# Attention on one core: the preparing transposes of keys and queries, and the products with the values, dealt anew over the nine loops of a head pair

## The chip, the cores and the metric

One Trainium2 chip, one core of it. The metric is device microseconds (us) of one execution of the whole program, lower is better. The kernel before took 1369.54 us, the median of three runs (1367.63 to 1370.73).

## The reference

The program computes three stages, one after the other: attention with pooled queries, a dense two-layer network with an ELU between the layers, and a routed network of eight experts. The change touches the attention alone:

```python
B, H, S, D = q.shape                                   # 4, 8, 1152, 64
q_pool = q.reshape(B, H, S // 2, 2, D).mean(axis=3)    # 576 queries per head
scores = 1/np.sqrt(D) * np.matmul(q_pool, k.transpose(0, 1, 3, 2))
scores = scores - np.max(scores, axis=-1, keepdims=True)
attn = np.exp(scores)
attn = attn / (np.sum(attn, axis=-1, keepdims=True) + 1e-09)
return np.matmul(attn, v).astype(np.float32)           # 1152 keys, 64 columns
```

## The kernel before, in words

**Pairs and tiles.** Two heads make a pair; there are 16 pairs (0 to 15). A pair has 2 x 576 queries, which are nine tiles of 128. Tiles 0 to 3 belong to the first head, tiles 5 to 8 to the second, and tile 4 is the middle tile, half of either. Every float32 factor is split into a high and a low part, so that products of float32 accuracy come out of several passes.

**One loop per tile.** The loop of lines 251 to 287 runs over all 144 tiles, nine loops to a pair; I write loop t for t = 0 to 8 within a pair. SEQ (line 17) is the order in which one loop emits its work, and since each engine takes its own instructions in that order, it also is each engine's order. One loop works at three depths:

- scores of the tile two ahead (`qk`, line 144; `q1` writes the last third of the keys to `Sb`, `q0` the first two thirds to `Sa`), their maxima on VectorE (`smax`, line 147, `nm<-Sb`, `nm<-Sa`; `bias`, line 150) and the exponentials on ScalarE (`exp`, line 154, `P<-Sa` and `P<-Sb`). A target tile 4 needs both heads' keys and so twelve products where the others need six; it is emitted in loop 2. `Sa` has one buffer in PSUM (CFG S2=1): the next `Sa` waits until the exponential has read the last one.
- the tile itself: its probabilities P are transposed in three groups of three (`tp`, line 187) into PSUM tiles `T`, and each group is taken out as a high part by ScalarE (`evH`, line 198, `PH<-T`) and a low part by VectorE (`evL`, line 200, `PL<-T,PH`). In loop 4, the middle tile, each takes two instructions for a group instead of one.
- products with the values of query chunks that are complete (`av`, line 210, `O<-PH,vs` and `O<-PL,vs`). A chunk has 18 of them, four chunks make 72 to a pair. AVN (line 18) says how many each loop emits. Loops 0 to 4 work on chunks of 256 columns, loops 5 to 8 on chunks of 320.

**What is prepared for the next pair.** The scores need transposed keys and queries. `kop` (lines 92 to 99) transposes a third of one head's keys: three transposes into a `T`, and one copy by ScalarE into `kst` (line 98). k00, k01, k02 are the thirds of the first head, k10, k11, k12 those of the second. `qop` (lines 101 to 118) does the same for thirds of the queries (line 105, copies in line 106), and after q2 two DMAs on SyncE's queue fill the second layout (lines 116, 117). PREP (line 19) says which of these each loop emits, late in its order (`prep`), behind the products with the values. The pair number there is relative: (0, ...) is this pair, (1, ...) the next. In loops 3 and 7 one more transpose follows, that of the inverse sums (`invT`, line 165, `T<-ident,rc`).

**The T buffers.** All of these, three P groups a loop, preparing thirds and `invT`, take their PSUM tile `T` from one pool of three buffers (CFG T=3) in turn. The fourth taken in a loop needs the first one's readers done, and so on.

**When the thirds are needed.** Loop 7 emits the first scores of the next pair (all k0 thirds and all q thirds), `Sb` first. Loop 2 emits the middle tile's scores, which need the k1 thirds: `Sb` with k12 first, then `Sa` with k10 and k11. Before, k12 is transposed at the end of loop 1 of its own pair.

**Extra work.** From the 71st loop on the loops also carry weight decoding for the next stage (lines 309 to 323, mostly VectorE), in pairs 8 to 12, and later splitting of its inputs.

Of the kernel before, what the change touches and what calls it, by code (L numbers as in the profile page):

```python
# [14 lines left out]


SEQ='q1 q0 m1 sum dec t0 c0 m0 pool scl t1 c1 bias l0 t2 av c2 l1 e0 e1 l2 aw prep inv st'.split()
AVN=(8,10,4,9,5,8,10,10,8)
PREP={0:((0,'k11'),(1,'q0')),1:((0,'k12'),),3:((1,'q1'),),4:((1,'q2'),(1,'k00'),(1,'k01')),5:((1,'k02'),),8:((1,'k10'),)}
POOL={0:((0,'vH1'),(0,'vL1')),1:((1,'kH0'),),2:((1,'kL0'),),4:((1,'kH1'),),5:((1,'kL1'),),6:((2,'qadd'),),7:((2,'qH'),(2,'qL')),8:((1,'vH0'),(1,'vL0'))}  # L20
SCALE=(7,8,11,12)
CFG=dict(S2=1,S1=2,T=3,O=1)
def attention(tc, q, k, v, xS, rS, ident, pairs=None, extra=(), start=lambda: None):
    nc=tc.nc
    B,H,S,D=q.shape
# [3 lines left out]
    with ctx:  # L29
# [4 lines left out]
        kv=ctx.enter_context(tc.tile_pool(name="a_kv",bufs=1))  # L34
# [53 lines left out]
        def prep_ops(i):  # L88

            d=D_[i]  # L90
            ops=[]
            def kop(h,g):
                def f():
                    if g==0: d['kst'][h]=kv.tile([128,S],F32R,name="kst",tag="kst",bufs=2)
                    T=psT.tile([128,384],F32,name="T",tag="T")
                    for j in range(3):
                        nc.tensor.transpose(T[:,j*128:(j+1)*128],d['ks'][h][:,3*g+j].rearrange("p a d -> p (a d)").bitcast(F32),ident)
                    nc.scalar.copy(out=d['kst'][h][:,g*384:(g+1)*384],in_=T)
                return f
            A=QA[i%2]; Bq=QB[i%2]  # L100
            def qop(g):
                def f():
                    T=psT.tile([128,384],F32,name="T",tag="T")
                    for j in range(3):
                        nc.tensor.transpose(T[:,j*128:(j+1)*128],d['qsp'][:,3*g+j].rearrange("p a d -> p (a d)").bitcast(F32),ident)
                    cp=lambda o,i: nc.scalar.activation(out=o,in_=i,func=AF.Copy,scale=SC)
                    if g==0: cp(A[:,0:384],T)
                    elif g==2: cp(A[:,896:1280],T)
                    else:
                        w=T.rearrange("p (c x) -> p c x",c=3)  # L110
                        cp(A[:,384:1152].rearrange("p (c x) -> p c x",c=2)[:,:,0:128],w[:,0::2])
                        cp(A[:,512:768].rearrange("p (y x) -> p y x",x=64)[:,0::3],w[:,1].rearrange("p (a x) -> p a x",a=2))

                    sl=(slice(0,384),slice(384,896),slice(896,1280))[g] if i==0 else slice(0,1280)
                    if g==2 or i==0:
                        nc.sync.dma_start(out=Bq[0:64,sl].bitcast(F32),in_=A[64:128,sl].bitcast(F32))
                        nc.sync.dma_start(out=Bq[64:128,sl].bitcast(F32),in_=A[0:64,sl].bitcast(F32))
                return f
            return {f'q{g}':qop(g) for g in range(3)}|{f'k{h}{g}':kop(h,g) for h in range(2) for g in range(3)}
# [77 lines left out]
        def evH(g,j):  # L197
            for H,L,src in parts(g,j): nc.scalar.copy(out=H,in_=src)  # L198
        def evL(g,j):
            for H,L,src in reversed(list(parts(g,j))): nc.vector.tensor_tensor(out=L,in0=src,in1=H.bitcast(F32),op=ALU.subtract)  # L200
# [28 lines left out]
        def do(i,*names):  # L229

            if i>=N: return
            if i not in ops: ops[i]=pool_ops(i,i==0)|prep_ops(i)
            for n in names:
                o=ops[i].pop(n,None)
                if o: o()
# [10 lines left out]
        def takeav(n):  # L246
            if avq:
                take(avq[0],n)
                if not avq[0]: avq.pop(0)
        stores=[]; sums={}  # L250
        for g in range(NG+4):
# [8 lines left out]
            for op in SEQ:  # L260
# [15 lines left out]
                elif a=='c': evH(g,int(n))  # L276
                elif op in ('av','aw'): takeav((AVN[t]+(op=='av'))//2)
                elif a=='l': evL(g,int(n))
                elif op=='sum':
                    if t in (3,7): ssum(i,t//4)  # L280
                elif op in ('pool','prep'):
                    for di,n in (POOL if op=='pool' else PREP).get(t,()): do(i+di,n)
                elif op=='dec':
# [706 lines left out]
```

## Time and profile before

| what | value |
|---|---|
| median of three runs | 1369.54 us |
| the profiled execution's own time | 1370.3 us |
| its span in the trace | 1368.5 us |
| PE (TensorE) busy, share of the span | 1242.2 us, 91% |
| PEld (weight loads, overlap PE) | 1098.8 us, 80% |
| DVE (VectorE) busy | 1099.7 us, 80% |
| ACT (ScalarE) busy | 907.4 us, 66% |
| POOL (GpSimd) busy | 625.6 us, 46% |

The attention's score products begin 12 us into the span and its last score maximum lies at about 584 us. Times of the trace are counted from the start of the span. A row of the timeline has its start, its length, the engine, the line of the kernel, the operation, the names that it writes and reads, and the number of like instructions that were merged; in brackets how long the engine was idle before it and who ended that. Matmuls are pipelined: their lengths overlap, and the distance from one start to the next is what each costs. In the text T(t) is the start of the nine transposes of loop t.

### The profile page before, as it was taken

How to read it: one execution, taken by the hardware profiler on the slowest of the kernel's cores; microseconds unless marked ns; L12 is line 12 of the kernel's file. 1: busy time of each engine (PE TensorE's matmuls, PEld its weight loads, DVE VectorE, ACT ScalarE, POOL GpSimd, SP SyncE). 2: the span in 40 equal slices, each digit the busy share in tenths (PEclk: the TensorE clock that was granted, in tenths of full speed). 3: DMA queues.
4: the chain of work that ended last, by engine and by line, in shares of the span. 5: the costliest groups of instructions: out<-in, count | busy, mean ns of one | idle time of the engine just before them, and what ended most of it. 6: DMA issues, size and time to landing. Idle time of an engine off the chain costs nothing. (4 is left out here: it accounts for less than half of the span.)

```text
span 1368.5 us, 22229 instructions
## 1 busy us (share of the span) xinstructions
PE 1242.2 (91%) x7476; PEld 1098.8 (80%) x7476; DVE 1099.7 (80%) x1970; ACT 907.4 (66%) x2104; POOL 625.6 (46%) x537
## 2 busy tenths in 40 slices
PE   5999999999999899977777999899989999999997
PEld 4988898888888888875565988797979887788885
DVE  5778887778888887879999497939395889998993
ACT  6888888887888788844444645454555666666772
POOL 4444444444444355336666543434342344545662
PEclk9999999999999999999999999999999999999998
DMA  5334333334443254233432311110100314348810
GB/s 157 98 106 107 106 107 106 103 100 114 113 113 105 83 142 113 62 118 94 127 99 73 110 32 35 32 34 22 33 24 17 154 50 159 100 161 326 298 35 21
DMA packets 78342, 136.62 MB, mean 100 GB/s; under 512 B 9255, under 2 KB 52663, under 8 KB 73872
## 3 DMA queue, kind: packets, MB, share of 16 engines
q1 hardware_dynamic: 73952, 123.22, 30.1%
q0 software_dynamic: 3696, 11.34, 2.4%
q8 instruction: 61, 1.00, 0.3%
q10 hardware_dynamic: 576, 0.59, 0.1%
q14 instruction: 57, 0.47, 0.1%
HBM read 155.48 MB, written 20.28 MB: 128 GB/s over the span
## 5 line engine op out<-in xcount | busy, mean ns | idle before, releaser
L399 PE MATMUL h<-xH,W 128*128 128x384 f32 (+1 forms) x896 | 229.2, 327 | 55.0 <-ACT yt L408 39.5
L198 ACT CAST PH<-T 128x384 fp32r<-128x384 f32 (+1 forms) x480 | 182.6, 460 | 94.5 <-PE T L187 92.5
L399 PEld LDWEIGHTS h<-xH,W 128*128 128x128 f32 x896 | 161.9, 195 | 77.0 <-ACT yt L408 50.2
L200 DVE TENSOR_TENSOR PL<-T,PH 128x384 fp32r<-128x384 f32 (+1 forms) x480 | 216.0, 509 | 1.3 <-ACT PH L198 1.3
L422 POOL TENSOR_TENSOR gL<-et,gH 128x384 fp32r<-128x384 f32 (+1 forms) x112 | 119.4, 1066 | 199.5 <-ACT gH L421 174.1
L787 DVE TENSOR_TENSOR W<-sg,W 128x2048 fp32r<-128x2048 f32 (+1 forms) x84 | 190.4, 2299 | 17.7 <-ACT W L786 9.8
L404 ACT ACTIVATE em<-h 128x384 f32<-128x384 f32 (+1 forms) x112 | 49.9, 445 | 224.9 <-DVE et L413 155.7
L210 PE MATMUL O<-PH,vs 128*128 128x256 f32 (+1 forms) x576 | 167.2, 313 | 0.6 <-ACT xo L213 0.6
L187 PE MATMUL T<-ident,P 128*128 128x128 f32 x1296 | 165.3, 273 | 0.0
L147 DVE TENSOR_REDUCE nm<-Sa 128x1 f32<-128x768 f32 x144 | 137.3, 954 | 29.7 <-PE Sa L144 18.6
L210 PE MATMUL O<-PL,vs 128*128 128x256 f32 (+1 forms) x576 | 157.6, 297 | 0.0
L187 PEld LDWEIGHTS T<-ident,P 128*128 128x128 f32 x1296 | 150.6, 141 | 5.1
L399 PE MATMUL h<-xL,W 128*128 128x384 f32 (+1 forms) x448 | 143.6, 321 | 0.0
L147 DVE TENSOR_REDUCE nm<-Sb 128x1 f32<-128x384 f32 x144 | 80.2, 557 | 72.8 <-PE Sb L144 72.2
L154 ACT ACTIVATE P<-Sa,bs 128x768 f32<-128x768 f32 x144 | 133.7, 929 | 7.0 <-DVE bs L150 6.6
L413 DVE SCALAR_TENSOR_TENSOR et<-em,et 128x384 f32<-128x384 f32 (+1 forms) x112 | 69.5, 621 | 83.9 <-ACT em L410 82.3
L144 PE MATMUL Sa<-kst,qa 128*128 128x384 f32 x320 | 111.1, 347 | 18.9 <-ACT P L154 18.8
L786 ACT CAST W<-sg 128x2048 fp32r<-128x2048 f32 (+1 forms) x63 | 114.3, 1836 | 12.7 <-DMA sg<-moe_w 12.7
L215 POOL TENSOR_TENSOR xo<-xo,rB 128x256 f32<-128x256 f32 (+1 forms) x64 | 52.2, 819 | 152.3 <-ACT xo L213 82.1
L430 PE MATMUL y<-W,gH 128*128 128x512 f32 x288 | 114.8, 398 | 0.0
L431 PE MATMUL y<-W,gH 128*128 128x512 f32 x288 | 113.2, 393 | 0.0
L210 PEld LDWEIGHTS O<-PH,vs 128*128 128x128 f32 x576 | 108.7, 189 | 1.1 <-ACT xo L213 0.8
(295 smaller groups left out, 3058.4 us busy)
## 6 DMA issues: line engine op xcount, KB each, us to landing
sg<-moe_w SPq DMA_DIRECT2D x80, 1024.0 KB
qb<-qa SPq DMA_DIRECT2D x30, 320.0 KB
qn<-q SPq DMA_DIRECT2D x16, 576.0 KB
kn<-k SPq DMA_DIRECT2D x16, 576.0 KB
rB<-rS SPq DMA_DIRECT2D x32, 288.0 KB
vn<-v SPq DMA_DIRECT2D x15, 576.0 KB
dx<-moe_w_in SPq DMA_DIRECT2D x16, 512.0 KB
dx<-moe_w_out SPq DMA_DIRECT2D x16, 512.0 KB
```

The lines of the kernel that those rows point to most:

```text
L147: nc.vector.tensor_reduce(out=s['nm'][:,n:n+1],in_=s['S'][n],axis=AX.XY if n==0 else AX.X,op=ALU.max,negate=True)
L154: nc.scalar.activation(out=o,in_=s['S'][n],func=AF.Exp,bias=s['bs'],scale=1.0,accum_out=s['su'][:,n:n+1])
L187: nc.tensor.transpose(T[:,n*128:(n+1)*128],P[:,kt*128:(kt+1)*128],ident)
L198: for H,L,src in parts(g,j): nc.scalar.copy(out=H,in_=src)
L200: for H,L,src in reversed(list(parts(g,j))): nc.vector.tensor_tensor(out=L,in0=src,in1=H.bitcast(F32),op=ALU.subtract)
L210: nc.tensor.matmul(O[0][:,:n],vs[:,kt].rearrange("p a d -> p (a d)"),R[:,kt,:n],start=first,stop=last)
L399: nc.tensor.matmul(h[:,:N],a,b[:,k,:N],start=(n==0),stop=(n==11)); n+=1
L422: nc.gpsimd.tensor_tensor(out=gL[:,:N],in0=t_,in1=gH[:,:N].bitcast(F32),op=ALU.subtract)
L430: nc.tensor.matmul(y,gH[:,sl],wH,start=(f==0),stop=False)
L431: nc.tensor.matmul(y,gH[:,sl],wL,start=False,stop=False)
L786: else: nc.scalar.copy(out=H[:,q],in_=s[:,q])
L787: (nc.gpsimd if (w,j,h) in self.pool_L else nc.vector).tensor_tensor(out=L[:,q],in0=s[:,q],in1=H[:,q].bitcast(F32),op=ALU.subtract)
```

## The change

PREP and AVN get other entries, and `kop` makes its `kst` tile at the first third that is emitted, whichever that is, since a pair's thirds no longer come in the order of their number.

```diff
-AVN=(8,10,4,9,5,8,10,10,8)
-PREP={0:((0,'k11'),(1,'q0')),1:((0,'k12'),),3:((1,'q1'),),4:((1,'q2'),(1,'k00'),(1,'k01')),5:((1,'k02'),),8:((1,'k10'),)}
+AVN=(7,11,0,5,13,8,10,9,9)
+PREP={0:((0,'k11'),(1,'q0')),1:((1,'q1'),),2:((1,'q2'),),3:((1,'k02'),(1,'k00')),5:((1,'k01'),),7:((1,'k12'),),8:((1,'k10'),)}
...
-                    if g==0: d['kst'][h]=kv.tile([128,S],F32R,name="kst",tag="kst",bufs=2)
+                    if h not in d['kst']: d['kst'][h]=kv.tile([128,S],F32R,name="kst",tag="kst",bufs=2)
```

By loops:

| loop | prepared before | prepared after | products with values before | after |
|---|---|---|---|---|
| 0 | k11, q0 | k11, q0 | 8 | 7 |
| 1 | k12 | q1 | 10 | 11 |
| 2 | none | q2 | 4 | 0 |
| 3 | q1 | k02, k00 | 9 | 5 |
| 4 | q2, k00, k01 | none | 5 | 13 |
| 5 | k02 | k01 | 8 | 8 |
| 6 | none | none | 10 | 10 |
| 7 | none | k12 | 10 | 9 |
| 8 | k10 | k10 | 8 | 9 |

## Rows read from the trace of the kernel before

**Rows 1.** Stretches: length, busy PE PEld DVE ACT POOL, granted clock, DMA share, GB/s

```profile
128.00:304.70 176.70, 166.50 (x1212) 156.35 (x1209) 140.95 (x305) 146.37 (x411) 74.91 (x77) 1.00 0.38 103
...
304.70:489.32 184.62, 169.22 (x1211) 156.43 (x1210) 155.00 (x326) 149.76 (x415) 81.62 (x78) 1.00 0.40 110
```

**Rows 2.** Waits from 15 to 584 us: total, times, longest

```profile
POOL qsp L65 <- PE T L105: 82.9, 11, 12.6
...
PE Sb L144 <- ACT kst L98: 14.2, 15, 1.0
...
PE T L105 <- DVE PL L200: 6.0, 17, 0.7
```

**Rows 3.** TensorE's timeline, pair 7, loops 1 to 3

```profile
273.16 1.14 PE L187 MATMUL T<-ident,P 128*128 128x128 f32 x9
...
275.80 0.33 PE L144 MATMUL Sb<-kst,qb 128*128 128x384 f32 x1
277.08 0.44 PE L144 MATMUL Sb<-kst,qa 128*128 128x384 f32 x1 [0.95 <-ACT kst L98]
...
278.92 1.15 PE L187 MATMUL T<-ident,P 128*128 128x128 f32 x9
...
281.64 0.44 PE L144 MATMUL Sa<-kst,qa 128*128 128x384 f32 x1 [0.76 <-ACT P L154]
...
282.44 1.14 PE L187 MATMUL T<-ident,P 128*128 128x128 f32 x9
283.34 0.36 PE L210 MATMUL O<-PH,vs 128*128 128x256 f32 x1
...
284.37 0.28 PE L210 MATMUL O<-PH,vs 128*128 128x256 f32 x1
284.49 0.49 PE L105 MATMUL T<-ident,qsp 128*128 128x128 f32 x3
...
284.84 0.42 PE L144 MATMUL Sb<-kst,qa 128*128 128x384 f32 x1
```

**Rows 4.** TensorE's timeline, pair 7, loops 4 and 5

```profile
285.98 1.14 PE L187 MATMUL T<-ident,P 128*128 128x128 f32 x9
...
288.02 0.52 PE L105 MATMUL T<-ident,qsp 128*128 128x128 f32 x3 [0.32 <-DVE PL L200]
288.55 1.05 PE L97 MATMUL T<-ident,ks 128*128 128x128 f32 x6
...
290.48 1.14 PE L187 MATMUL T<-ident,P 128*128 128x128 f32 x9
```

**Rows 5.** TensorE's timeline, pair 0, scores of the middle tile

```profile
28.30 0.34 PE L144 MATMUL Sb<-kst,qb 128*128 128x384 f32 x1
28.48 0.34 PE L144 MATMUL Sb<-kst,qa 128*128 128x384 f32 x1
```

**Rows 6.** ScalarE's timeline, pair 7, loops 2 and 4

```profile
279.45 1.25 ACT L198 CAST PH<-T 128x384 fp32r<-128x384 f32 x3 [2.42 <-PE T L187]
...
281.36 0.22 ACT L154 ACTIVATION_READ_ACCUMULATOR P<-Sa,bs 128x1 f32 x1
...
288.57 0.25 ACT L154 ACTIVATION_READ_ACCUMULATOR P<-Sa,bs 128x1 f32 x1
```

**Rows 7.** VectorE's timeline, pair 7, loops 3 and 4

```profile
281.58 0.55 DVE L147 TENSOR_REDUCE nm<-Sb 128x1 f32<-128x384 f32 x1
...
282.64 0.96 DVE L147 TENSOR_REDUCE nm<-Sa 128x1 f32<-128x768 f32 x1
...
283.71 1.48 DVE L200 TENSOR_TENSOR PL<-T,PH 128x384 fp32r<-128x384 f32 x3
...
287.25 1.68 DVE L200 TENSOR_TENSOR PL<-T,PH 128x192 fp32r<-128x192 f32 x6
```

**Rows 8.** Stretches again: loop 4 of pair 7, and an early stretch of pair 0

```profile
285.90:289.40 3.50, 3.16 (x26) 2.54 (x24) 2.85 (x9) 3.19 (x14) 0.67 (x1) 1.00 0.14 48
...
19.00:26.00 7.00, 4.60 (x24) 3.73 (x23) 4.56 (x9) 3.96 (x10) 6.61 (x7) 0.81 0.57 188
```

## The prediction

> **What bounds the kernel now.** I read the stretches first. Five pairs without extra work, pairs 3 to 7, take 176.70 us, 35.34 a pair; TensorE is busy for 166.50 of it, VectorE for 140.95, ScalarE for 146.37 [rows 1]. So TensorE is the bound, and what it loses shows in two places. The list of waits names them: `Sb` on ScalarE's `kst` copy, 15 times 0.95, and query transposes on VectorE's `PL`, 17 times [rows 2]. The timeline of one pair shows where. In loop 2 the second `Sb` product starts at 275.80 and the third, which needs k12, at 277.08 [rows 3]: k12 was transposed just before, and its copy stands behind two exponentials on ScalarE. In loop 4 the transposes of q2 sit idle until VectorE has freed a T buffer, and the six of k00 and k01 behind them take 1.05 [rows 4]. A third wait, of `Sa` on the exponential (281.64), is no queue but the loop's own chain [rows 3].
>
> **The change, by stretches from T(t) to T(t+1).** Nothing is added or removed in number: nine preparing thirds and 72 products a pair stay; what changes is which wait ends last.
>
> *Loop 1 to 2.* Before, 275.80 to 278.92, 3.12 for eleven starts [rows 3]. Where the second head's keys were ready, in pair 0, the same two `Sb` products follow at 0.18 (28.30, 28.48) [rows 5]; eleven starts at 0.175 are 1.92. The wait and its restart give 1.20. q1 replaces k12 at the same three transposes. One product of 256 columns more: 283.34 to 284.37 is eight distances, the first longer, 0.115 for the others [rows 3], so +0.11. Sum -1.09. Its cover: k12 now is copied from loop 7 on, four loops ahead; k10 and k11 one loop at least.
>
> *Loop 2 to 3.* 3.52 now, and it stays, though loop 2 loses all four products. `Sa` here waits for ScalarE: evictions from 279.45, T(2)+0.53, then the exponential, whose sum is read at 281.36 for 0.22, and `Sa` at 281.64, T(2)+2.72 [rows 3, 6]. The four products only filled that wait, and q2 now fills it. Its buffer is freed by the first of three `PL`: these begin 1.27 behind T and last 1.48 together (283.71, loop 3), so the first ends near T+1.8, the second T+2.3, the third T+2.75 [rows 7]; in loop 4 TensorE started some 0.14 behind such an end (six halves from 287.25, the second of them over near 287.88, q2 at 288.02) [rows 4, 7]. So q2 starts at T+1.95, takes 0.27, two `Sb` starts take 0.43: T+2.65, under 2.72. q2's two DMAs on SyncE's queue go with it and have five loops until loop 7. GpSimd gains: its `qsp` copy waits for q2's transposes, 82.9 us in all [rows 2], and would now be let go two loops sooner; nobody waits for that. 0, with 0.07 to spare; +0.2 if the DMA wait or the copy behind q2 held ScalarE.
>
> *Loop 3 to 4.* The price of the change. T(3) to the first `Sb` was 2.40 (282.44 to 284.84) [rows 3]. Now five products are out by T+1.56, k02 waits for the first `PL`, k00 for the second, and `invT`, the sixth T of this loop, for the third: T+2.75, +0.14, +0.03 to the `Sb`, T+2.92. So +0.52. Low end +0.30 (TensorE goes on right behind k00, T+2.42 and 0.27); high end +0.75, if the maximum of `Sb`, which follows q2 now, pushes the `Sa` maximum (281.58 and 282.64 before, with the sums between [rows 7]) by the 0.2 that its `Sb` comes later. I take 0.52: it follows rows of the same loop.
>
> *Loop 4 to 5.* 4.50 before (285.98 to 290.48) [rows 4]: three preparing thirds behind halved evictions. Now none, and 13 products: 0.90 for the nine transposes, 0.20 + 11 x 0.115, 0.12 to the `Sb`, 0.43 for it, T+2.92; ScalarE releases `Sa` by 288.57 + 0.25, T+2.84 to 2.90 [rows 6]. A tie; then 0.70 (0.80 if it waited) for `Sa`: 3.62 to 3.70. I take 3.65, -0.85. Cover: with no preparing third, nothing on TensorE waits for the six halves until the next loop's T.
>
> *Loop 7 to 8* takes k12 beside `invT`: four transposes in place of one, 0.35 for four (284.49 to 284.84) less 0.03, so +0.32; one product of 320 columns less, 0.115 x 320/256 = 0.14. +0.18. `invT` waits for the second `PL`, T+2.42, and comes near T+2.5 anyway. *Loop 8 to 0* one such product more: +0.14. *Loop 0 to 1* one product less, but q0 waits for the second `PL` there: 0, at best -0.11. Loops 5 and 6: k01 for k02, 0.
>
> A pair: -1.09 + 0.52 - 0.85 + 0.18 + 0.14 = **-1.10**; from its ends -1.48 to -0.6.
>
> **The sum.** Pairs 1 to 7, 13 and 14: 9 x 1.10 = 9.9. Pairs 8 to 12 take 184.62 where 5 x 35.34 = 176.70 would do [rows 1]: VectorE has the decoding too, and part of that hides now in the very waits that go (loops 2 and 4). I take 0.7 a pair, 3.5, between 0 and 5.5. Pair 15 prepares nothing and has only the first gain, 1.2. Pair 0 never waited for k12; its loops 3, 4, 7 and 8 cancel: 0. Together 14.6. What follows the attention is paced by its own work and shifts. The profiled execution took 1370.3 (span 1368.5); 1370.3 - 14.6 = 1355.7. The median of the runs is 0.76 lower, so 1354.9: **1355**.
>
> **A rule that speaks against it.** In loop 4 before, 18 transposes and five value products made 3.16 busy of 3.50, and the granted clock stayed 1.00, the 2.4 GHz level; between 19 and 26 us, where TensorE was busy for 4.60 of 7.00, it was 0.81, so partly at 1.2 [rows 8]. The Trainium skill (TensorE: Matmul & The Clock Gate, Part 4: PE-mode transpose) says that transposes do not count as TensorE activity as other matmuls do, so that they do not bring the full clock. By that rule the new loops 2 and 3, 28 transposes beside five value products, could fall to the lower level; the loop 4 of before, with more transposes to a product, does not bear it out. By that rule the time would be the one of the third rival below.
>
> **Rivals.**
> 1. *The waits come back on VectorE or ScalarE.* Per pair ScalarE is busy for 29.3 of 35.3 and VectorE for 28.2 [rows 1]; with TensorE's idle stretches gone, the chain maximum, exponential, `Sa` (2.72 + 0.80 = 3.52 a loop) may bind in more loops, and loop 3 goes to its high end. For it: the 3.52 that loop 2 already shows. Against: the other loops are past it by TensorE's work alone. Half the gain, 7 us: 1362.
> 2. *The third buffer does not bind in loop 3* (+0.30), and loops 0 and 4 reach their better ends: 1.48 a pair, 14 pairs 20: 1349. Against it: in loop 4 of before, the last third waited just so.
> 3. *The other side: the clock.* Between T(2) and T(4) 28 transposes, 12 score and 5 value products cost 28 x 0.11 (nine take 0.90 to the next start, 282.44 to 283.34 [rows 3]) + 12 x 0.175 + 5 x 0.115 = 5.7 of 7.57 us. At half the clock they take 5.7 more, of which some 1.9 fits into idle time: +3.8 a pair, 2.7 net, 14 pairs 38: 1408. It decides from about 30% of that stretch at the lower level, a granted clock there under 0.85. For it: the 0.81 early on; against: 1.00 through loop 4 [rows 8].
> 4. *It does not do what it says*: some third still is late, for instance k02 in loop 3 on GpSimd's split of the keys, and a wait of 1 us stands elsewhere: 1369.5.
>
> **How the numbers follow.** Forecast 0.62 (own range 1351 to 1359), first rival 0.20, second 0.08, clock 0.04, no gain 0.06. About 0.2%, 2.7 us, is what a measurement of this kernel can tell from no change. Faster: 0.62 + 0.20 + 0.08 less a little of the first rival, 0.88; same 0.06; slower 0.06. The range takes in the first rival and the second: 1348 to 1364.
>
> **What would show it.** Right: `Sb` on `kst` gone from the waits; T(1) to T(2) near 4.67, T(4) to T(5) near 3.65; `T<-ident,rc` of loop 3 waiting for `PL`, T(3) to T(4) near 4.06; a pair near 34.25. Wrong: T(2) to T(3) over 3.6, q2 having eaten its 0.07; T(3) to T(4) over 4.3; a granted clock under 0.95 after 51 us; or a later stage that gives the time back by waiting for its loads.

## The result, and the profile after

The changed kernel takes 1348.75 us (median of four runs, 1347.96 to 1349.12) against 1369.26 for the kernel before beside it (1367.63 to 1370.73): a ratio of 0.985, 95% interval 0.9833 to 0.9867. It is 20.5 us faster where 14.6 were forecast, some 6 us beyond the forecast and 0.75 us inside the range. The last maximum of `Sa` comes at 563.0 us in place of 583.8, so 20.8 of the span's 21.2 us were won in the attention; what follows moved with it, 784.7 us before and 784.3 after.

The page after, busy time and share of the span, beside the table of before:

```profile
span 1347.3 us, 22234 instructions
...
PE 1235.9 (92%) x7476; PEld 1093.2 (81%) x7476; DVE 1100.8 (82%) x1970; ACT 906.2 (67%) x2104; POOL 625.8 (46%) x537
```

The same work, in less time. The waits after, from 15 to 584 us (who waited for whom, total, times, longest):

```profile
PEld T L105 <- DVE PL L200: 15.4, 16, 1.0
...
PE T L105 <- DVE PL L200: 11.8, 17, 0.7
...
POOL qsp L65 <- PE T L105: 6.6, 1, 6.6
...
PEld T L165 <- DVE PL L200: 2.7, 16, 0.3
```

The 15 waits of `Sb` for a `kst` copy [rows 2] are not in this list any more. GpSimd waits 6.6 us for query transposes, not 82.9. In their place q2 waits for VectorE in loop 2 (0.72 each time), and the inverse-sum transpose, line 165, for the third low part in loop 3: the two waits that the prediction named. TensorE's timeline of pair 7, to be read against [rows 3] and [rows 4]:

```profile
267.33 1.14 PE L187 MATMUL T<-ident,P 128*128 128x128 f32 x9
...
269.58 0.49 PE L105 MATMUL T<-ident,qsp 128*128 128x128 f32 x3
269.82 0.42 PE L144 MATMUL Sb<-kst,qa 128*128 128x384 f32 x1
...
270.25 0.34 PE L144 MATMUL Sb<-kst,qa 128*128 128x384 f32 x1
...
271.99 1.14 PE L187 MATMUL T<-ident,P 128*128 128x128 f32 x9
273.86 0.55 PE L105 MATMUL T<-ident,qsp 128*128 128x128 f32 x3 [0.72 <-DVE PL L200]
274.16 0.42 PE L144 MATMUL Sb<-kst,qa 128*128 128x384 f32 x1
...
275.50 1.14 PE L187 MATMUL T<-ident,P 128*128 128x128 f32 x9
...
277.46 0.92 PE L97 MATMUL T<-ident,ks 128*128 128x128 f32 x6 [0.23 <-POOL qsp L67]
278.30 0.27 PE L165 MATMUL T<-ident,rc 128*5 128x128 f32 x1
278.33 0.42 PE L144 MATMUL Sb<-kst,qa 128*128 128x384 f32 x1
...
279.47 1.14 PE L187 MATMUL T<-ident,P 128*128 128x128 f32 x9
...
283.17 1.14 PE L187 MATMUL T<-ident,P 128*128 128x128 f32 x9
```

The third `Sb` product of loop 2 now follows at 270.25 without a gap. From T to T: 4.66, 3.51, 3.97, 3.70, where before stood 5.76, 3.52, 3.54, 4.50. (The label GpSimd at 277.46 is the last semaphore seen; k02 starts T+1.96, where the freed T buffer was expected, T+1.95.)

Stretches after, columns as in [rows 1]: five pairs with decoding (8 to 12), the plain attention, and the early stretch of [rows 8]:

```profile
296.35:470.95 174.60, 167.21 (x1212) 156.34 (x1211) 152.29 (x326) 149.30 (x415) 79.44 (x77) 1.00 0.41 117
```

```profile
51.00:255.00 204.00, 198.24 (x1447) 186.80 (x1446) 168.29 (x364) 174.42 (x489) 88.79 (x90) 1.00 0.40 107
19.00:26.00 7.00, 5.48 (x20) 4.63 (x19) 3.70 (x7) 2.45 (x6) 6.46 (x7) 0.53 0.55 187
```

A plain pair takes 34.20 us (35.36 before). Pairs 8 to 12 take 174.60 where they took 184.62 [rows 1]: 10.0 us less, when five plain pairs would gain 5.8. That is where the result leaves the forecast.

### The profile page after: what moved, and what is told of

Read it like the earlier page. It is cut to its first block, busy times and chain, and to the rows that moved or that the text cites. A ratio compares the mean times of both kernels' runs of the same rounds, so it can differ in the third digit from the quotient of the medians.

```text
span 1347.3 us, 22234 instructions
## 1 busy us (share of the span) xinstructions
PE 1235.9 (92%) x7476; PEld 1093.2 (81%) x7476; DVE 1100.8 (82%) x1970; ACT 906.2 (67%) x2104; POOL 625.8 (46%) x537
## 5 line engine op out<-in xcount | busy, mean ns | idle before, releaser
L399 PE MATMUL h<-xH,W 128*128 128x384 f32 (+1 forms) x896 | 224.9, 322 | 57.6 <-ACT yt L408 41.6
L399 PEld LDWEIGHTS h<-xH,W 128*128 128x128 f32 x896 | 158.1, 191 | 80.6 <-ACT yt L408 52.7
L787 DVE TENSOR_TENSOR W<-sg,W 128x2048 fp32r<-128x2048 f32 (+1 forms) x84 | 193.4, 2336 | 14.6 <-POOL W L785 7.4
L210 PE MATMUL O<-PH,vs 128*128 128x256 f32 (+1 forms) x576 | 161.9, 305 | 0.6 <-ACT xo L213 0.6
```

The source lines that it names most:

```text
L210: nc.tensor.matmul(O[0][:,:n],vs[:,kt].rearrange("p a d -> p (a d)"),R[:,kt,:n],start=first,stop=last)
L399: nc.tensor.matmul(h[:,:N],a,b[:,k,:N],start=(n==0),stop=(n==11)); n+=1
L787: (nc.gpsimd if (w,j,h) in self.pool_L else nc.vector).tensor_tensor(out=L[:,q],in0=s[:,q],in1=H[:,q].bitcast(F32),op=ALU.subtract)
```

## The experiments

"Plain" stretches are the medians of pairs 1 to 6, taken from one start of the `Sa` maximum to the next; "the loss with decoding" is what pairs 7 to 14 take together beyond eight plain pairs (7.9 us before, 3.6 after). Runs 1 to 8 were timed once each, 9 and 10 four times.

**1. k12 early, and nothing else.**

```diff
 # against the kernel before
-PREP={0:((0,'k11'),(1,'q0')),1:((0,'k12'),),3:((1,'q1'),), ... 8:((1,'k10'),)}
+PREP={0:((0,'k11'),(1,'q0')),3:((1,'q1'),), ... 7:((1,'k12'),),8:((1,'k10'),)}
```

> The kernel before with one edit: k12 is transposed in loop 7 of the pair before instead of loop 1 of its own; products and all else stay. My theory, steps that add: T(1) to T(2) falls from 5.76 to 4.55, T(7) to T(8) grows from 3.57 to 3.72 to 3.89 (three transposes, 0.33, beside the inverse sums), all other loops stay; a pair 35.36 to about 34.4, the whole 1.0 x 15 shorter, near 1355. On the decoding in pairs 8 to 12, which cost 7.8 us beyond five plain pairs before and 3.6 after: if that loss came through the wait for k12 (VectorE late, exponentials late, the copy of k12 behind them late), it falls here to 5 or less; if it comes from GpSimd working at the same time as VectorE's two-input instructions, it stays near 7.8, since q2 and with it GpSimd's order stay, and VectorE's decoding stays near 17.5 us.

Measured: 1349.39 us in one run, beside 1370.25 before. A plain pair is 34.14 us, even below the 34.20 of the whole change. TensorE's timeline of pair 7, T(1) to T(5), with the waits that are left:

```profile
266.05 1.15 PE L187 MATMUL T<-ident,P 128*128 128x128 f32 x9
...
270.27 1.14 PE L187 MATMUL T<-ident,P 128*128 128x128 f32 x9
...
272.99 0.44 PE L144 MATMUL Sa<-kst,qa 128*128 128x384 f32 x1 [0.75 <-ACT P L154]
...
273.79 1.15 PE L187 MATMUL T<-ident,P 128*128 128x128 f32 x9
...
277.31 1.15 PE L187 MATMUL T<-ident,P 128*128 128x128 f32 x9
...
279.36 0.52 PE L105 MATMUL T<-ident,qsp 128*128 128x128 f32 x3 [0.31 <-DVE PL L200]
...
281.82 1.15 PE L187 MATMUL T<-ident,P 128*128 128x128 f32 x9
```

T(1) to T(2) is 4.22, not the 4.55 expected: I had left out that loop 1 then prepares nothing, 0.24 less on TensorE (three transposes took that from 269.58 to 269.82 in the changed order); the other 0.09 is not explained. Nearly all of the gain of the change is in this one edit: from the end of pair 0 to the last maximum its attention is 0.8 us longer than in the changed kernel. In the plain pairs the rest of the change nets +0.06 us each: -0.81 in the stretch from loop 4 to 5 and -0.15 from 7 to 8, against +0.44 from 1 to 2 (q1 and one product), +0.44 from 3 to 4 and +0.15 from 8 to 0. On the decoding, VectorE's part fell to 14.5 us, where the theory of GpSimd wanted 17.5, and the loss to 5.6, between the 5 of the one theory and the 7.8 of the other.

**2. All but k12.**

```diff
 # against the changed kernel
-PREP: 1:((1,'q1'),),
-PREP: 7:((1,'k12'),),
+PREP: 1:((0,'k12'),(1,'q1')),
```

> The changed kernel with one edit back: k12 is transposed again in loop 1 of its own pair, ahead of q1. Steps that add: T(1) to T(2) back at 5.76 or a little over, T(7) to T(8) at 3.52 to 3.57; T(3) to T(4) stays 3.97, T(4) to T(5) stays 3.70; a pair near 35.0, and the whole near 1362. Rival, that the wait for k12 is filled by the transposes of q1 behind it: a pair near 34.5, since q1 would stand behind k12 and take time that was idle. Decoding: by the GpSimd theory its cost is as after (3.6, VectorE's decoding near 14.6 us), since q2 is in loop 2; by the theory that it came through the wait for k12 it is near 7.

Measured: 1364.22 us in one run; a plain pair 34.99, stretches as the steps said (5.76, 3.51, 3.96, 3.69; loop 7 to 8 3.47). Pair 7, T(1) to T(2):

```profile
270.01 1.15 PE L187 MATMUL T<-ident,P 128*128 128x128 f32 x9
...
272.26 0.49 PE L97 MATMUL T<-ident,ks 128*128 128x128 f32 x3
272.59 0.49 PE L105 MATMUL T<-ident,qsp 128*128 128x128 f32 x3
...
273.92 0.44 PE L144 MATMUL Sb<-kst,qa 128*128 128x384 f32 x1 [0.49 <-ACT kst L98]
...
275.77 1.15 PE L187 MATMUL T<-ident,P 128*128 128x128 f32 x9
```

The wait is 0.49 in place of 0.95, since q1 and a product more stand in it, but its end has not moved: these are free here and cost 0.44 once k12 is early. So the parts do not add: -0.37 and -1.22 a pair alone, -1.16 together. The loss with decoding was 7.3, VectorE's decoding 18.3 us; the theory of GpSimd, that q2's place alone sets this, had said 3.6 and 14.6, and failed a second time.

**3 and 4. The decoding behind the attention**, in the kernel before and in the changed one.

```diff
-attention(tc,q,k,v,xS,rS,ident,extra=pre,start=norms)
+attention(tc,q,k,v,xS,rS,ident,start=norms)
+for o in pre: o()
```

> The kernel before, with the weight decoding and splitting that ride in pairs 8 to 15 emitted behind the attention instead. The attention alone is looked at, by the last maximum of Sa (583.8 us before); the whole gets longer, by 10 to 60 us, since that work then stands alone. If all of pairs 8 to 12's extra is decoding: pairs 8 to 12 take 5 x 35.36 and the last maximum comes at 576.0. If something else slows these pairs: later than 578.

> The changed kernel, with the weight decoding and splitting emitted behind the attention instead. Pairs 8 to 12 take 5 x 34.20, the last maximum of Sa comes at 559.4 (563.0 after), 16.6 before that of the same edit in the kernel before; so 4.2 of the 20.8 us that the attention gained came from the decoding's lower cost. Rival: the plain pairs gain as much as the others when nothing rides in them, and the difference is 20 or more.

Measured: the last `Sa` maximum at 575.7 and 559.8 us; pairs 8 to 12 like the plain ones (within 0.2 us over five) in both. (The wholes are 1417.26 and 1400.91, since the decoding then stands alone.) So all of that loss is decoding, and of the 20.8 us won in the attention 16.0 are there without it; some 4.8 came with it, 4.3 of them as the smaller loss, the rest by how long pair 0 happened to take in each run.

**5 and 6. The decoding four loops earlier**, in the kernel before and in the changed one.

```diff
-want=NX*max(0,g-70)//max(1,NG-74)
+want=NX*max(0,g-66)//max(1,NG-74)
```

> The kernel before with the decoding begun four loops earlier, so that each of its instructions falls into another loop; plain pairs stay 35.36. Theory, that the loss in the pairs with decoding is set by how many of VectorE's decoding instructions meet GpSimd at work: VectorE's decoding time and the loss move together; between 14.5 and 18.5 us and 3.5 and 8 (in the four kernels so far 14.5 and 5.5, 14.6 and 3.6, 17.5 and 7.8, 18.3 and 7.4), and they differ from 17.5 and 7.8 by over 1. Rival, that the order of the kernel before loses more in itself, whatever meets: 7.8 again, within 0.7.

> The changed kernel with the decoding begun four loops earlier; plain pairs stay 34.20. Theory of the meetings: VectorE's decoding time and the loss move together and leave 14.6 and 3.6 by over 1 in the loss, to 5 or more if the time is 16 or more. Rival, that the changed order loses less in itself: 3.6 again, within 0.7.

Measured: 1373.49 and 1348.6 us, one run each. VectorE's decoding 15.8 us and a loss of 10.0 in the kernel before (17.5 and 7.9 as shipped); 14.5 and 5.2 in the changed one (14.6 and 3.6). The sum of VectorE's decoding time does not order the losses, as that theory wanted; that an order loses a fixed amount is wrong as well. This does not show that the meetings with GpSimd cost nothing: behind the next table the traces show that they do. From these runs I formed the theory of the next two.

**7 and 8. The same shift with k12 alone early, and with all but k12.** The edit is that of 5 and 6, in the kernels of 1 and 2.

> The kernel of k12_only (k12 early, three preparing thirds still in loop 4) with the decoding begun four loops earlier. I sum, over pairs 7 to 14, what each of the nine stretches takes beyond its plain length. Theory, that the decoding's delays of VectorE reach TensorE through the two waits themselves: the stretch from loop 4 to 5 loses +1.05 within 0.25, as in all three kernels so far with three preparing thirds in loop 4 (1.07, 1.05, 1.06; without them -0.41 to -0.66); the stretch from loop 1 to 2 loses nothing (0.0 or less), as in the five kernels so far without the wait for k12. Rival, that these sums are a matter of where each decoding instruction falls: with all of them in other loops, either sum comes out on the other side.

> The kernel of all_but_k12 (k12 late, no preparing third in loop 4) with the decoding begun four loops earlier. Theory of the two waits: the stretch from loop 4 to 5 gains, -0.4 to -0.7; the stretch from loop 1 to 2 loses +0.3 or more (1.55, 1.47 and 0.37 in the three kernels with the wait for k12). Rival, where each instruction falls: either comes out on the other side.

Measured: 1351.24 and 1364.83 us, one run each, and all four sums as the theory of the two waits had them. What pairs 7 to 14 lose beyond plain length, in us, worked out from the starts of the `Sa` maxima of each trace:

```
order            decoding    k12    thirds in loop 4   loop 1 to 2   loop 4 to 5   all nine
before           as shipped  late   three                 1.55          1.07        7.86
before           4 earlier   late   three                 0.37          1.05       10.03
all but k12      as shipped  late   none                  1.47         -0.66        7.33
all but k12      4 earlier   late   none                  0.34         -0.55        6.03
k12 alone early  as shipped  early  three                -0.44          1.06        5.58
k12 alone early  4 earlier   early  three                -0.36          1.04        8.79
changed          as shipped  early  none                 -0.66         -0.61        3.57
changed          4 earlier   early  none                 -0.45         -0.54        5.19
```

Counted so, taking the three thirds out of loop 4 is worth 1.6 to 1.7 us in the stretch from loop 4 to 5 in all four comparisons; k12 early is worth 2.0 and 2.1 in the stretch from 1 to 2 with the decoding as shipped, 0.7 and 0.8 with it shifted. But these two stretches do not make the whole: with k12 late, the kernel without thirds in loop 4 loses as shipped only 0.5 us less than the kernel before (7.33 against 7.86). And the mark is VectorE's own: the `Sa` maximum stands behind a decoding instruction, so part of such a difference is the maximum's own delay. Counted by TensorE's starts T, the thirds are worth 0.8 to 0.9 us in loop 4 in all four comparisons, and k12 early 1.5 and 1.7 us in loops 1 and 2 together as shipped, 1.1 and 0.6 shifted.

Counted by T, the largest part lies in loop 0, which neither wait touches: as shipped it loses 2.4 us in the kernel before and 1.9 with k12 alone early, against 0.4 in the changed one and 0.5 with all but k12. GpSimd, VectorE and TensorE in loop 0 of pair 10, before:

```profile
377.02 1.43 POOL L67 TENSOR_TENSOR ks<-kn,ks 128x576 fp32r<-128x576 f32 x1
...
377.30 1.70 DVE L315 SCALAR_TENSOR_TENSOR dx<-dx 128x512 int32<-128x512 int32 x1
...
377.32 1.14 PE L187 MATMUL T<-ident,P 128*128 128x128 f32 x9
...
382.53 1.15 PE L187 MATMUL T<-ident,P 128*128 128x128 f32 x9
```

and after:

```profile
367.38 0.68 DVE L315 SCALAR_TENSOR_TENSOR dx<-dx 128x512 int32<-128x512 int32 x1
...
367.41 1.14 PE L187 MATMUL T<-ident,P 128*128 128x128 f32 x9
...
368.68 0.87 POOL L215 TENSOR_TENSOR xo<-xo,rB 128x320 f32<-128x320 f32 x1 [3.04 <-DMA rB<-rS]
...
371.60 1.15 PE L187 MATMUL T<-ident,P 128*128 128x128 f32 x9
```

The same instruction takes 1.70 us beside GpSimd and 0.68 without it, and T(0) to T(1) is 5.21 in place of 4.19 (3.83 plain). In all ten kernels that decode in the attention, whatever the order, a loop 0 with decoding in it is longer than plain by the decoding time in it less 0.31 to 0.33 us (0.42 us cost 0.10, 0.68 cost 0.36, 1.74 cost 1.42), and that time exceeds 0.68 only in the four kernels where q2 stands in loop 4 and GpSimd with it is late. So 2.0 of the 4.3 us come from GpSimd's new place in time, 0.8 from the three thirds in loop 4, where 0.68 us of decoding cost 0.36 with three thirds, 0.11 with one (run 9) and nothing with none. The 1.7 of loops 1 and 2 are not separated: k12 is early there, but the two decoding instructions of loop 2 also took 1.0 and 0.9 us in place of 1.9 each. The other loops lose 0.2 more together.

Most of what the shifted kernels lose in loop 0 (4.36 us in the kernel before, in the table's way of counting) is no decoding at all. In pair 13 TensorE waits there for the queries, since GpSimd had stood 23 us before the data of the splitting, which the shift also starts earlier:

```profile
490.28 1.00 POOL L375 TENSOR_TENSOR dx<-dx 128x384 f32<-128x384 f32 x1 [23.09 <-DMA dx<-xS]
...
495.79 0.55 PE L105 MATMUL T<-ident,qsp 128*128 128x128 f32 x3 [2.39 <-POOL qsp L67]
```

That loop is 3.3 us longer than plain, and 2.3 in the kernel of run 7.

**9 and 10. Two versions that the steps point to.** First, k00 in loop 4, where one third and nine products fit in front of ScalarE's release:

```diff
 # against the changed kernel
-AVN=(7,11,0,5,13,8,10,9,9)
-PREP: 3:((1,'k02'),(1,'k00')),
+AVN=(7,11,0,9,9,8,10,9,9)
+PREP: 3:((1,'k02'),),4:((1,'k00'),),
```

> The changed kernel with k00 transposed in loop 4 instead of loop 3, and the products of the first chunk dealt 9 and 9 over loops 3 and 4 instead of 5 and 13. It tests the price of the third T buffer in loop 3. If the inverse-sum transpose waits there for VectorE's last low part: T(3) to T(4) falls from 3.97 to 3.52, T(4) to T(5) stays 3.70, since ScalarE sets its end and one third and nine products (T+2.28 to the Sb) still fit in front; a pair 34.20 to 33.76, the whole 6.5 shorter, near 1342. Rival, that any preparing third in loop 4 waits for the halved low parts: T(4) to T(5) at 4.0 or more, a pair near 34.1 and no change of the whole.

Then, on top of it, four of loop 1's products in loop 2, AVN=(7,7,4,9,9,8,10,9,9):

> As the run with k00 in loop 4, and four of the eleven products of loop 1 moved to loop 2, which has none now. q2 waits in loop 2 for the first low part (T+1.95) in any case, so four products (T+1.46) are free there; loop 1 is then set by q1's wait for its T buffer: T(1) to T(2) falls from 4.66 to 4.36, T(2) to T(3) stays 3.51; a pair near 33.45, the whole near 1338. Rival, that the 0.07 to spare in loop 2 is gone: T(2) to T(3) at 3.8, and a pair stays near 33.76.

Measured: 1343.13 us (four runs, ratio to before 0.9811, 0.9795 to 0.9827), a plain pair 33.77; and **1340.15 us** (four runs, 0.979, 0.9773 to 0.9806), a plain pair 33.45. T(3) to T(5) of the first, in pair 7:

```profile
271.50 1.14 PE L187 MATMUL T<-ident,P 128*128 128x128 f32 x9
...
275.02 1.15 PE L187 MATMUL T<-ident,P 128*128 128x128 f32 x9
...
277.06 0.52 PE L97 MATMUL T<-ident,ks 128*128 128x128 f32 x3
...
278.71 1.15 PE L187 MATMUL T<-ident,P 128*128 128x128 f32 x9
```

and T(1) to T(3) of the second:

```profile
261.96 1.14 PE L187 MATMUL T<-ident,P 128*128 128x128 f32 x9
...
266.30 1.14 PE L187 MATMUL T<-ident,P 128*128 128x128 f32 x9
...
268.17 0.55 PE L105 MATMUL T<-ident,qsp 128*128 128x128 f32 x3 [0.25 <-DVE PL L200]
...
269.83 1.15 PE L187 MATMUL T<-ident,P 128*128 128x128 f32 x9
```

3.52 and 3.69, and 4.34 and 3.53: both as expected to 0.02 us. The third T taken beside two thirds was the price in loop 3, and the four products are free in loop 2, where q2's wait shrinks from 0.72 to 0.25 and its end stays. The second whole is 2 us over the expected 1338: its loss with decoding is 6.2, not 3.6. By TensorE's starts 1.6 of that is in loop 4 of pairs 8 and 12, where the decoding fell beside GpSimd again: 1.23 and 1.47 us long in place of 0.42 and 0.68, it cost 0.67 and 0.90.

## Why the prediction was right, and by how much its size was off

- *Loop 1 to 2*, forecast -1.09: measured 5.76 to 4.66, -1.10. Its price is shown by runs 1 and 2: k12 early is -1.22 a pair alone, and with q1 and a product more in front of it the wait ends at the same place.
- *Loop 2 to 3*, forecast unchanged with 0.07 to spare: 3.52 and 3.51. q2 started T+1.87 where T+1.95 was expected, the `Sb` T+2.17.
- *Loop 3 to 4*, forecast +0.52: +0.43 to +0.44. The inverse-sum transpose starts T+2.80, not T+2.89. Run 9 takes its third place in the queue of buffers away and the price is gone.
- *Loop 4 to 5*, forecast -0.85: -0.80. The new length, 3.70, is ScalarE's release of `Sa`, the upper of the two values given; in run 9 four products fewer and a third more leave it at 3.69.
- *Loops 7, 8 and 0*, forecast +0.18, +0.14 and 0: 3.57 to 3.75, 3.54 to 3.69, 3.83 and 3.83.
- *A pair*: forecast -1.10, measured -1.16 (the better end of the forecast adds up to -1.46, not -1.48). Nine plain pairs: 9.9 forecast, 10.5 measured. Pair 15: 1.2 forecast, 27.06 to 25.81, 1.25 measured.
- *Pair 0*: forecast 0; with the start it took 1.0 longer (19.32 + 34.48 to 19.87 + 34.93). The early stretch from 19 to 26 us shows a granted clock of 0.53 where it was 0.81 [rows 8], so mostly the lower level; T(0) came 1.2 us later. This is no effect of the change that the runs show: pair 0, which moving the decoding does not touch, ended at 53.8, 53.7 and 55.8 us in three runs of the order before, and at 54.8, 55.1 and 52.5 in three of the changed one.
- *Pairs 8 to 12* are the term that was mis-sized: "VectorE has the decoding too, and part of that hides now in the very waits that go (loops 2 and 4). I take 0.7 a pair, 3.5, between 0 and 5.5." Measured 10.0, above even the upper end. Two steps failed. The sign of that argument was wrong in loop 4: the wait for VectorE's low parts was no room in which the decoding hid, but the place where it reached TensorE (0.36 of each 0.68 us, nothing once the thirds were gone; 0.8 us in all). And the forecast put GpSimd's earlier release at nothing, "nobody waits for that": it took GpSimd's splits away from the decoding in loop 0, which is worth 2.0 us. Of the 1.7 us in loops 1 and 2, how much came through the wait for k12 stays open.

So it is by luck that the range held the result: the forecast's own range ended at 1351, and 1348.75 lies where the second rival stood, at 1349, though what that rival said of the third buffer did not come about.

Against the rivals: the waits did not come back on VectorE or ScalarE beyond the two that were priced (first rival); the third buffer did bind (second); the granted clock was 1.00 from 51 to 255 us, with the 28 transposes beside five products in loops 2 and 3 of every pair (third). So the rule of the Trainium skill on transposes and the clock (TensorE: Matmul & The Clock Gate, Part 4: PE-mode transpose) did not bear on these stretches. The fourth had a wait of 1 us standing elsewhere: none did in the plain pairs, where the longest is q2's 0.72, in a stretch that stayed at 3.51.

What the forecast did not say, though its own terms held it, is that the parts of the change other than k12's place cancel: -0.85 for loop 4 against what q1, the third buffer and the products cost in loops 1, 3, 7 and 8.

## What to carry to other kernels

Before a wait is priced, mark who sets its end: a chain that runs through another engine passes on what that engine's extra work exceeds its slack by (here 0.36 of 0.68 us in loop 4), so removing the wait can be worth more in the stages where that engine is busiest. An engine that nobody waits for can still cost time by when it works: moving q2 moved GpSimd away from VectorE's decoding. Work put in front of a wait is free only while the wait stands, so parts of an edit that are each worth something can cancel once the wait is gone; the cheapest single edit is worth a run of its own. Where buffers are taken in turn, count the takers of a loop: the fourth, fifth and sixth wait for the first, second and third reader, and one of them moved to a loop with fewer takers gave 0.44 us a pair here.

## What the runs showed of the hardware that was not expected

VectorE's decoding instructions, in which all operands lie in SBUF, took much longer when GpSimd was at work. In the kernel before, GpSimd and VectorE near 461 us:

```profile
461.28 1.43 POOL L67 TENSOR_TENSOR ks<-kn,ks 128x576 fp32r<-128x576 f32 x1
462.65 1.88 POOL L67 TENSOR_TENSOR qn<-qn 128x576 f32<-128x576 f32 x1
```

```profile
461.30 1.95 DVE L313 SCALAR_TENSOR_TENSOR dx<-dx 128x512 int32<-128x512 int32 x1
```

and the same line after, with GpSimd idle beside it:

```profile
317.58 0.68 DVE L313 SCALAR_TENSOR_TENSOR dx<-dx 128x512 int32<-128x512 int32 x1
```

1.95 against 0.68 us. The Trainium skill (SBUF — State Buffer, SBUF: two separate sides) describes a port pair that VectorE and GpSimd hold in turn for a whole instruction; this agrees with it. The single-input line 311 was drawn out too, from 0.42 to as much as 1.67 us. The sum of these lengths, 14.5 to 18.3 us over ten kernels, does not order the losses by itself, since the loops pass on different shares of it.

The granted clock between 19 and 26 us differs from run to run of the same order: 0.81, 0.85 and 0.50 in three runs of the order before, 0.53, 0.50 and 0.76 in three of the changed one, 1.00 and 0.50 in two with all but k12. So the order of work alone does not set it.
